# Where a skipped branch's DMAs are issued, and when three bonus terms are: an RWKV and Sinkhorn-MoE kernel on one Trainium2 core

## The chip, the cores and the metric

The kernel runs on one core of one Trainium2 chip. The metric is the device time of one execution in microseconds (us), lower being better; several executions are timed and their median is compared. One further execution is recorded by the hardware profiler. The engines are TensorE (PE, matmuls; its weight loads are PEld), VectorE (DVE), ScalarE (ACT), GpSimd (POOL) and SyncE (SP, which here only issues DMAs). Each engine works through its own instructions in order and waits on semaphores that the others, or landing DMAs, count up.

## The reference

The first half is an RWKV-like recurrence over 768 steps for 4 batches, 8 heads and a head size of 48; the second half a mixture of 8 experts whose gate is normalized by eight Sinkhorn rounds.

```python
def _attn_ref(r, k, v, w, u):
    state = zeros((B, H, D, D))
    for t in range(S):
        cur = einsum('bhd,bhe->bhde', u[None] * kt, vt)
        y[:, :, t] = einsum('bhd,bhde->bhe', rt, state + cur)
        state = w[None, :, :, None] * state + einsum('bhd,bhe->bhde', kt, vt)

def _moe_ref(x, w_gate, w1, w2):          # x: 3072 x 384
    P = exp(x @ w_gate - max)
    for _ in range(8):
        P /= P.sum(1, keepdims=True) + 1e-09
        P /= P.sum(0, keepdims=True) + 1e-09
        P *= N / E
    for e in range(E):
        out += P[:, e:e + 1] * (maximum(x @ w1[e], 0.0) @ w2[e])
```

The decay w is drawn between 0.85 and 0.95.

## The kernel before

**The tiles.** The 3072 tokens are 24 tiles of 128, six to a batch. In the recurrence a tile is one chunk: within it the recurrence becomes a masked matrix product with powers of w, and a state S (48 x 48 per head) is carried from chunk to chunk. For tile tt the code issues these steps, always in the order in which they stand in the text, since every engine is wrapped so that its instructions keep program order:

- `prep` (line 522): POOL scales r to `rp`, DVE scales k to `kp`.
- `bonus_dot` (528): POOL multiplies r by k and by u into `rk`.
- `stage_b` (547): PE transposes rp and kp (`prT`, `pkT`), ACT copies them to `rT` and `kT`.
- `stage_c` (558): PE makes the scores `pA`, DVE copies them under the mask into `at` (COPY_PREDICATED); then PE makes the chunk's state part `pu`, DVE adds it into S, and POOL multiplies S by the chunk's decay `wbd` (two instructions; not in a batch's first chunk).
- `bonus` (537): DVE reduces rk to `dg`, POOL multiplies v by it (into the same buffer, still named rk) and adds `xadd(tt)`, a part of `hbx` that holds zeros unless the branch below has filled it.
- `stage_d` (602): PE makes the output `py`, DVE adds the bonus to give x, takes its largest value and a power-of-two scale.
- `emit` (775): ACT and DVE split x into two fp16 halves (`xsc`), and SP issues a DMA transpose into `hbx`, from where the expert matmuls (`pht`) read it.

**The weights.** `load_part` and `load_w1` issue loads on SP's queue; w1 of the first expert comes in three pieces of 512 KB. DVE takes each piece's largest value (`wm`); a scale follows over PE (`pmax_w`), and ACT and DVE split the weights into two fp16 parts (`ws`). These pieces of work are put in between by `steps(n)`. `spin(n)` issues n filler matmuls on zeros (`pz`).

**The branch.** The closed form is used for channels whose w lies between 0.7 and 1.1. Others are counted in `flag`, and `with tc.If(bad > 0)` (line 487) runs `scan_channels` (443), a loop over all 768 steps that fills `xadd`. With the inputs of this case no channel is outside and the body is never run. Still its DMAs are part of the program: one of w, seven in the loop, and 24 that read `xadd` back, all on SP's queue. Every engine passes the branch on its own: it loads the flag (line 486) and compares (487). For instructions that come later, the body counts as a writer of `xadd`.

**The order at the head.** Lines 791 to 858 issue tiles 0 to 3 by hand, with weight steps and the first expert matmuls in between; from line 860 on a loop goes over the other tiles. In lines 816 to 849 each of the tiles 1 to 3 is issued as `state_of`, `stage_c`, `bonus`; in the loop `bonus` stands ahead of `stage_c`. The expert stages (14 half experts, from line 1294 on) follow.

Of the kernel before, what the change touches and what calls it, by code (L numbers as in the profile page):

```python
# [32 lines left out]
def rwkv_sinkhorn_moe(  # L33
# [13 lines left out]
    V, S_, G, T, Q = (  # L47
        InOrder(tc, e) for e in (nc.vector, nc.scalar, nc.gpsimd, nc.tensor, nc.sync)
    )

    B, H, S, D = r.shape
# [34 lines left out]
    def part(home, dtype, at, shape):  # L86

        n = 1
        for s_ in shape:
            n *= s_  # L90
        x_ = home if home.dtype == dtype else home.bitcast(dtype)
        x_ = x_[:, at : at + n]
        if len(shape) == 1:
            return x_
        names = "abcd"[: len(shape)]
        return x_.rearrange(
            f"p ({' '.join(names)}) -> p {' '.join(names)}", **{c_: s_ for c_, s_ in zip(names[1:], shape[1:])}
        )
# [14 lines left out]
    def xadd(t):  # L113
        return part(hbx, F32, t * DM, (DM,))
# [163 lines left out]
    def whole(gen):  # L278
        leave()
        for _ in gen:  # L280
            pass
# [23 lines left out]
    def spin(n):  # L305
        pz = ps2.tile([P, TB], F32, tag="po", name="pz")
        for _ in range(n):
            T.matmul(pz, zeros[:, :P], zeros, start=True, stop=True)
# [4 lines left out]
    def load_part(tt, nm, src):  # L313
        b, c = divmod(tt, NCHB)
        if tt == 3 and nm != "v":
            t_ = part(hb3, F32, HB + "rk".index(nm) * H * D, (H, D))
        else:
            t_ = ld.tile([P, H, D], F32, tag=nm + "n", name=f"{nm}n_{tt}", bufs=5 if nm == "v" else 3)
        Q.dma_start(t_, src[b, :, c * C : (c + 1) * C, :].rearrange("h t d -> t h d"))
        loads.setdefault(tt, {})[nm] = t_  # L320
# [9 lines left out]
    def load_w1(c):  # L330
        Q.dma_start(raws[0][:, c], w1[0, c * P : (c + 1) * P, :])

    for tt in range(2):
        load_part(tt, "r", r)
        load_part(tt, "k", k)
    load_w1(0)
    load_w1(1)
    load_part(0, "v", v)
    Q.dma_start(
        ub.rearrange("p h d -> p (h d)"),  # L340
        u.rearrange("(o h) d -> o (h d)", o=1).broadcast_to([P, H * D]),
    )
    load_w1(2)
    load_part(1, "v", v)
    load_part(2, "r", r)
# [97 lines left out]
    def scan_channels(scratch):  # L443

        BH = B * H
        yd = scratch.tile([B, S, DM], F32, name="yd")
        rows = [part(hbx, F32, i * BH * D, (BH, D))[:D] for i in range(4)]
        kb, rb, stt, kv = rows
        wn, wbad, wz = (part(hbx, F32, 4 * BH * D + i * H * D, (H * D,))[:D] for i in range(3))
        vt, yv = (part(hbx, F32, 5 * BH * D + i * BH, (BH,))[:D] for i in range(2))  # L450
        Q.dma_start(wn, w.rearrange("(o h) d -> o (h d)", o=1).broadcast_to([D, H * D]))
        V.tensor_scalar(wbad, wn, W_MAX, W_MIN, op0=ALU.min, op1=ALU.max)
        V.tensor_tensor(wbad, wn, wbad, op=ALU.not_equal)
        V.memset(wz, 0.0)
        V.copy_predicated(wz, wbad.bitcast(I32), wn)
        V.memset(stt, 0.0)

        def of_b(x_):
            return x_.rearrange("p (b h) d -> p b (h d)", b=B)

        def for_b(x_):
            return x_.unsqueeze(1).broadcast_to([D, B, H * D])

        with tc.For_i(0, S, 1) as t:
            for dst, src in ((kb, k), (rb, r)):
                Q.dma_start(
                    dst,
                    src.rearrange("b h s d -> s (b h) d")[bass.ds(t, 1)].broadcast_to([D, BH, D]),
                )
            Q.dma_start(vt, v.rearrange("b h s d -> s d (b h)")[bass.ds(t, 1)].rearrange("o d a -> (o d) a"))  # L470
            V.tensor_tensor(rb, rb, stt, op=ALU.mult)
            V.tensor_reduce(yv, rb, axis=AX.X, op=ALU.add)
            for b in range(B):
                Q.dma_start(
                    yd[b].rearrange("s (h d) -> s d h", d=D)[bass.ds(t, 1)].rearrange("o d h -> (o d) h"),
                    yv[:, b * H : (b + 1) * H],
                )
            V.tensor_tensor(of_b(kb), of_b(kb), for_b(wbad), op=ALU.mult)
            V.tensor_tensor(kv, kb, vt.unsqueeze(2).broadcast_to([D, BH, D]), op=ALU.mult)
            V.tensor_tensor(of_b(stt), of_b(stt), for_b(wz), op=ALU.mult)  # L480
            V.tensor_tensor(stt, stt, kv, op=ALU.add)
        yt = yd.rearrange("b s d -> (b s) d").rearrange("(t p) d -> p t d", p=P)
        for t in range(NTT):
            Q.dma_start(xadd(t), yt[:, t, :])

    bad = nc.values_load(flag.bitcast(I32), min_val=0, max_val=0x44000000)
    with tc.If(bad > 0):
        with tc.tile_pool(name="scratch", bufs=1, space=bass.MemoryType.DRAM) as scratch:
            scan_channels(scratch)
# [17 lines left out]
    def gate_across():  # L507
        res = over_partitions(wgm, 1, ps1, "ph", "wg")
        next(res)
        return res  # L510
# [26 lines left out]
    def bonus(tt):  # L537
        vn = loads[tt]["v"]
        dg = at2.tile([P, H], F32, tag="dg", name=f"dg_{tt}")
        V.tensor_reduce(dg, st[tt]["rk"], axis=AX.X, op=ALU.add)  # L540
        av = st[tt].pop("rk")
        G.tensor_tensor(av, vn, dg.unsqueeze(2).broadcast_to([P, H, D]), op=ALU.mult)
        aq = av.rearrange("p h d -> p (h d)")
        G.tensor_tensor(aq, aq, xadd(tt), op=ALU.add)
        st[tt]["av"] = av

    def stage_b(tt):
        d = st[tt]
        for nm, src in (("rT", rp_[tt % 2]), ("kT", kp_[tt % 3])):
            pt = ps3.tile([P, NPAIR, P], F32, tag="pa", name=f"p{nm}_{tt}")  # L550
            sv = src.rearrange("p (a j) d -> p a (j d)", j=2)
            for p_ in range(NPAIR):
                T.transpose(pt[:, p_, :], sv[:, p_, :], ident)
            dst = at2.tile([P, NPAIR, P], F32, tag=nm, name=f"{nm}_{tt}", bufs=3 if nm == "rT" else 2)
            S_.copy(dst, pt)
            d[nm] = dst
# [197 lines left out]
    def work(n, ready=True):  # L754
        if not ready:
            spin(3)
            return
        for _ in range(n):
            if units:
                whole(units.pop(0))  # L760
# [19 lines left out]
    def steps(n):  # L780
        for _ in range(n):
            prepare()
# [4 lines left out]
    def state_of(tt):  # L787
        if ("S", tt) in st:
            st[tt]["S"] = st.pop(("S", tt))
# [23 lines left out]
    gate_max()  # L813
    steps(2)
    spin(3)
    state_of(1)
    stage_c(1)
    bonus(1)
    gate_res = gate_across()
    emit(0)  # L820
    steps(2)
# [7 lines left out]
    gate_split(gate_res)  # L829
    stage_b(3)  # L830
    work(1)
    state_of(2)
    stage_c(2)
    bonus(2)
    work(1)
    emit(1)
    steps(3)
# [6 lines left out]
    stage_d(2)  # L844
    stage_b(4)
    work(1)
    state_of(3)
    stage_c(3)
    bonus(3)
    work(1)  # L850
    steps(1)
    emit(2)
# [489 lines left out]
```

## Time and profile before

| what | value |
|---|---|
| time, median of 3 executions | 1570.2 us (1569.58 to 1573.74) |
| time of the profiled execution | 1572.32 us |
| its span | 1570.6 us, 26412 instructions |
| busy: PE, DVE, ACT, POOL | 97%, 66%, 42%, 38% |
| mean granted clock of PE | 0.985 |
| DMA | 143.14 MB, mean 91 GB/s |

Busy shares are those of the span. In a timeline row stand start, duration, engine, line, operation, output and inputs by the program's names, shape, count, and in brackets the idle time of the engine before it and who ended that. Since the helper class records every instruction, nearly all have the line L29 and are told apart by their names. SPq, POOLq and so on are an engine's sequencer, which issues DMAs and handles branches and semaphores. In a row of waits stand the total, the number and the longest. "Landing" is the time from a DMA's issue to its end.

### The profile page before, as it was taken

Reading aid. Unit: us, or ns where it says so; the run is one execution under the profiler, and the core shown is the slowest. Engines: PE = TensorE matmul, PEld = TensorE weight load, DVE = VectorE, ACT = ScalarE, POOL = GpSimd, SP = SyncE. Lnnn points to the kernel's source line nnn. Section 1 sums busy time; section 2 is a strip of 40 time slices with the busy share of each in tenths; the row PEclk is TensorE's granted clock in tenths of the full one; section 3 lists DMA queues with packets and bytes.
Section 4 is the critical chain, followed back from the end, with each engine's and each line's share of the span. In section 5 each row is a group of like instructions: output and inputs, shape, how many; then the busy total and the mean of one; then the engine's idle time right before and its main releaser. Section 6 shows DMA issues by size and latency. Waiting matters only on the chain.

```text
span 1570.6 us, 26412 instructions
## 1 busy us (share of the span) xinstructions
PE 1526.4 (97%) x10435; PEld 869.3 (55%) x10435; DVE 1029.6 (66%) x1715; ACT 663.6 (42%) x1164; POOL 596.9 (38%) x712
## 2 busy tenths in 40 slices
PE   6689999999999999999999999999999999999999
PEld 3666676555555555555555555555555555555555
DVE  6568877867656666666666666766666666656554
ACT  3133342444535454444445454545444444535320
POOL 5557997601022424334242425242333424242200
PEclk8799999999999999999999999999999999999999
DMA  7244551321135566666666666564545554555434
GB/s 182 52 93 103 109 118 49 107 81 39 56 100 106 60 89 123 89 126 90 118 86 122 89 119 96 79 109 60 96 58 98 59 96 60 96 60 96 56 91 131
DMA packets 186846, 143.14 MB, mean 91 GB/s; under 512 B 109536, under 2 KB 180960, under 8 KB 186720
## 3 DMA queue, kind: packets, MB, share of 16 engines
q0 software_dynamic: 44928, 61.36, 31.8%
q1 hardware_dynamic: 141584, 80.07, 18.6%
q8 instruction: 82, 1.34, 0.4%
q14 instruction: 44, 0.36, 0.1%
q10 hardware_dynamic: 208, 0.00, 0.0%
HBM read 55.39 MB, written 80.23 MB: 86 GB/s over the span
## 4 chain that ended last, share of the span: by engine, by line
PE 89%; DVE 4%; POOL 4%; issue 1%; ACT 0%; DMA 0%; POOLq 0%; DVEq 0%
PE po L29 46%; PE bZ L29 11%; PE bY L29 11%; PE bA L29 5%; PE bB L29 5%; PE ph L29 4%; PE bC L29 2%; POOL rk L29 2%; PE py L29 1%; PE pA L29 1%; PE pht L29 1%; POOL ws L29 1%; POOL rp L29 1%; DVE ws L29 1%; DVE hb L29 0%
## 5 line engine op out<-in xcount | busy, mean ns | idle before, releaser
L29 PE MATMUL po<-ws,hbx 128*128 128x384 f16 x3360 | 736.8, 326 | 0.0
L29 POOL DMA_DIRECT2D accd<-stg x288 | 250.4, 870 | 694.9 <-ACT stg L29 676.5
L29 PEld LDWEIGHTS <-hbx 128*128 128x128 f16 x3504 | 334.1, 98 | 292.5
L29 PEld LDWEIGHTS <-ws 128*128 128x128 f16 x3240 | 312.4, 100 | 243.9 <-issue 5.4
L29 PE MATMUL po<-ws,hb 128*128 128x384 f16 x1248 | 327.0, 330 | 5.4 <-ACT ws L29 2.5
L29 ACT ACTIVATE hbx<-tb 128x512 f16<-128x512 f32 x224 | 141.1, 630 | 449.6 <-DVE tb L29 449.6
L29 DVE TENSOR_TENSOR tb<-bY,tb 128x512 f32<-128x512 f32 x168 | 116.2, 692 | 195.7 <-PE bY L29 195.5
L29 ACT ACTIVATE stg<-po,pe 128x384 f32<-128x384 f32 x312 | 179.4, 575 | 121.9 <-PE po L29 95.1
L29 PE MATMUL bZ<-xv,ws 128*128 128x512 f16 x840 | 227.0, 379 | 0.4 <-DVE tb L29 0.4
L29 PE MATMUL bY<-xv,ws 128*128 128x512 f16 x840 | 227.0, 379 | 0.0
L29 DVE TENSOR_TENSOR tb<-bZ,tb 128x512 f32<-128x512 f32 x168 | 115.6, 688 | 135.6 <-PE bZ L29 135.6
L29 PEld LDWEIGHTS <-hb 128*128 128x128 f16 x1248 | 122.2, 99 | 101.5 <-issue 7.9
L29 POOL TENSOR_TENSOR ucb<-rawb 128x256 f32<-128x256 f32 x84 | 75.4, 948 | 117.1 <-DMA rawb<-in_moe_w_dram 117.1
L29 DVE TENSOR_TENSOR tb<-bB,tb 128x512 f32<-128x512 f32 x112 | 77.5, 692 | 49.1 <-PE bB L29 47.2
L29 PE MATMUL ph<-hbx,ws 128*128 128x384 f16 x504 | 93.1, 330 | 3.1 <-DMA hbx<-xsc 2.5
L29 DVE SCALAR_TENSOR_TENSOR hb<-tb,hbx 128x512 f16<-128x512 f32 x112 | 77.2, 690 | 24.6 <-ACT hbx L29 19.5
L29 PE MATMUL bA<-xv,ws 128*128 128x512 f16 x336 | 90.8, 379 | 0.0
L29 PE MATMUL bB<-xv,ws 128*128 128x512 f16 x336 | 90.8, 379 | 0.0
L29 DVE SCALAR_TENSOR_TENSOR hbx<-tb,hbx 128x512 f16<-128x512 f32 x112 | 77.9, 696 | 14.7 <-ACT hbx L29 10.4
L29 ACT COPY tb<-bZ 128x512 f32<-128x512 f32 x56 | 32.8, 586 | 65.4 <-PE bZ L29 65.4
L29 ACT COPY stg<-po 128x384 f32<-128x384 f32 x48 | 22.9, 477 | 72.0 <-PE po L29 62.9
L29 DVE TENSOR_REDUCE wms<-rawb 128x1 f32<-128x768 f32 x56 | 51.8, 944 | 0.0
(171 smaller groups left out, 1538.0 us busy)
## 6 DMA issues: line engine op xcount, KB each, us to landing
accd<-stg POOLq DMA_DIRECT2D x288, 192.0 KB, 3.7
rawb<-in_moe_w_dram SPq DMA_DIRECT2D x28, 768.0 KB, 7.2
e0d<-stg SPq DMA_DIRECT2D x48, 192.0 KB, 2.1
hb<-e0d SPq DMA_DIRECT2D x48, 192.0 KB, 3.9
vn<-in_v_dram SPq DMA_DIRECT2D x24, 192.0 KB, 3.3
accd<-stg SPq DMA_DIRECT2D x24, 192.0 KB, 1.8
accd<-hb POOLq DMA_DIRECT2D x24, 192.0 KB, 4.8
rawb<-accd SPq DMA_DIRECT2D x24, 192.0 KB, 2.5
```

The lines of the kernel that those rows point to most:

```text
L29: return lambda *a, **k: self.tc.keep_in_program_order(f(*a, **k))
```

## The change

Three things are changed. All DMAs of the branch body go by GpSimd's queue (`G`) in place of SP's (`Q`). In the loads ahead of the branch, u (`ub`) and v of tile 0 are issued before the second piece of w1. And for tiles 1 to 3 `bonus` is issued before `state_of` and `stage_c`.

```diff
     load_w1(0)
-    load_w1(1)
-    load_part(0, "v", v)
     Q.dma_start(
         ub.rearrange("p h d -> p (h d)"),
         u.rearrange("(o h) d -> o (h d)", o=1).broadcast_to([P, H * D]),
     )
+    load_part(0, "v", v)
+    load_w1(1)
     load_w1(2)
...
-        Q.dma_start(wn, w.rearrange("(o h) d -> o (h d)", o=1).broadcast_to([D, H * D]))
+        G.dma_start(wn, w.rearrange("(o h) d -> o (h d)", o=1).broadcast_to([D, H * D]))
...
             for dst, src in ((kb, k), (rb, r)):
-                Q.dma_start(
+                G.dma_start(
...
-            Q.dma_start(vt, v.rearrange("b h s d -> s d (b h)")[bass.ds(t, 1)].rearrange("o d a -> (o d) a"))
+            G.dma_start(vt, v.rearrange("b h s d -> s d (b h)")[bass.ds(t, 1)].rearrange("o d a -> (o d) a"))
...
             for b in range(B):
-                Q.dma_start(
+                G.dma_start(
                     yd[b].rearrange("s (h d) -> s d h", d=D)[bass.ds(t, 1)].rearrange("o d h -> (o d) h"),
...
         for t in range(NTT):
-            Q.dma_start(xadd(t), yt[:, t, :])
+            G.dma_start(xadd(t), yt[:, t, :])
...
     spin(3)
+    bonus(1)
     state_of(1)
     stage_c(1)
-    bonus(1)
     gate_res = gate_across()
```

Tiles 2 and 3 are changed as tile 1 is, with `bonus` now behind `work(1)` and ahead of `state_of`.

SP's instructions around the branch, of before (-) and after (+), its start; the semaphores in brackets are what an instruction waits for, DMAHW0 to 7 being those of the DMAs that SP and ACT issue:

```order
 L486 TENSOR_LOAD flag [waits DVE_49]
 L487 COMPARE_AND_BRANCH
-L29 DMA hbx<-in_w_dram 48x384 [waits DMAHW4_49,Activation_49]
 L464 COMPARE_AND_BRANCH
-L464 UNCONDITIONAL_BRANCH [waits DMAHW0_49,DMAHW1_49,DMAHW2_49,DMAHW3_49,DMAHW5_49,DMAHW6_49,DMAHW7_49]
```

The body's DMA of w, and with it the waits on the other seven semaphores, leave SP's program; the body's 31 others go in the same way.

POOL's instructions from the bonus of tile 0 to the state of tile 1, with their waits (rk_233 is the buffer of tile 0, rk_348 of tile 1, rk_431 of tile 2; DMASW0 to 7 are the semaphores of the DMAs that POOL issues):

```order
 L29 TENSOR_TENSOR rk_233<-vn_121,dg_387 128x384 [waits DMAHW0_49,DVE_49]
-L29 TENSOR_TENSOR rk_233<-rk_233,hbx 128x384 [waits DMAHW5_49,DMAHW4_49,Pool_49]
-L29 TENSOR_TENSOR rp_197<-rn_127,rtab 128x8x48 [waits PE_49]
-L29 TENSOR_TENSOR rk_431<-rn_127,kn_129 128x384
+L29 TENSOR_TENSOR rk_233<-rk_233,hbx 128x384 [waits DMASW1_49,DMASW0_49,Pool_49]
+L29 TENSOR_TENSOR rp_197<-rn_127,rtab 128x8x48 [waits DMAHW4_49,PE_49]
+L29 TENSOR_TENSOR rk_431<-rn_127,kn_129 128x384 [waits DMAHW5_49]
 L29 TENSOR_TENSOR rk_431<-rk_431,ub 128x384 [waits Pool_49]
+L29 TENSOR_TENSOR rk_348<-vn_125,dg_483 128x384 [waits DMAHW3_49,DVE_49]
+L29 TENSOR_TENSOR rk_348<-rk_348,hbx 128x384 [waits DMASW1_49,Pool_49]
 L29 TENSOR_TENSOR S_205<-S_205,wbd 64x4x48 [waits DVE_49]
 L29 TENSOR_TENSOR S_205<-S_205,wbd 64x4x48 [waits DVE_49,Pool_49]
```

The add of `xadd(0)` (a part of hbx) waits on two of POOL's own DMA semaphores in place of two of SP's, and the two bonus instructions of tile 1 now stand ahead of the state's.

DVE's instructions of tile 1 (at_203 holds its masked scores, S_205 its state; mt_wg and md_wg belong to the gate's scale):

```order
 L29 RECIPROCAL sw_323<-isw_322 128x1
-L29 COPY_PREDICATED at_203<-mask,pA_0_483 128x4x128
-L29 COPY_PREDICATED at_203<-mask,pA_1_484 128x4x128
-L29 TENSOR_TENSOR S_205<-pu_503,S_204 64x4x48 x2
-L29 TENSOR_REDUCE dg_516<-rk_348 128x8
+L29 TENSOR_REDUCE dg_483<-rk_348 128x8
+L29 COPY_PREDICATED at_203<-mask,pA_0_487 128x4x128
+L29 COPY_PREDICATED at_203<-mask,pA_1_488 128x4x128
+L29 TENSOR_TENSOR S_205<-pu_507,S_204 64x4x48 x2
 L29 TENSOR_REDUCE mt_wg<-pmax_wg 1x1
```

The reduce to dg moves from behind the mask copies and the state to ahead of them; in tiles 2 and 3 the same happens.

More of the change, by code (lines that the diff above doesn't have):

```diff
@@ L831, in rwkv_sinkhorn_moe @@
     work(1)
+    bonus(2)
     state_of(2)
     stage_c(2)
-    bonus(2)
     work(1)
@@ L846, in rwkv_sinkhorn_moe @@
     work(1)
+    bonus(3)
     state_of(3)
     stage_c(3)
-    bonus(3)
     work(1)
```

## The prediction

> **What bounds the kernel now.** I read the page first, for where TensorE (PE) is not busy; then the waits of PE by stretches of time; then the timeline of the first 75 us. All times are us from the start of the span.
>
> ```profile
> PE   6689999999999999999999999999999999999999
> ...
> PE prT L29 <- POOL rp L29: 20.2, 4, 8.2
> PE pkT L29 <- DVE kp L29: 2.1, 1, 2.1
> ...
> PE prT L29 <- POOL rp L29: 3.9, 3, 2.0
> ...
> 200.00:300.00 100.00, 99.91 (x1197) 67.67 (x1195) 77.02 (x152) 38.19 (x71) 77.94 (x89) 1.00 0.39 97
> ```
>
> One digit is 39 us. PE is the bound from the third digit on, and in the window of 200 to 300 us it is busy 99.91 of 100. So only time that PE loses at the head can be won. The first two wait rows are for 20 to 75 us: PE waits 20.2 us in four pieces for POOL's `rp` (the scaled r of the next tile, transposed by `prT`). The third row is for 75 to 200 us and is small: 3.9.
>
> The largest piece is 8.2. The timeline shows what POOL did before it:
>
> ```profile
> 16.35 0.83 POOL L29 TENSOR_TENSOR rk<-vn,dg 128x384 f32<-128x384 f32 x1 [0.51 <-DVE dg L29]
> 17.99 1.05 SPq L29 DMA_DIRECT2D vn<-in_v_dram  x1
> 18.49 1.90 PE L29 MATMUL py<-vn,at 128*64 128x48 f32 x32
> 26.58 0.99 POOL L29 TENSOR_TENSOR rk<-rk,hbx 128x384 f32<-128x384 f32 x1 [9.40 <-SPq L487]
> 27.53 1.00 POOL L29 TENSOR_TENSOR rp<-rn,rtab 128x384 f32<-128x384 f32 x1
> 28.58 1.11 PE L29 MATMUL prT<-ident,rp 128*128 128x128 f32 x4 [8.19 <-POOL rp L29]
> ...
> L487 SPq EVENT_SEMAPHORE  x8: 17/17/17, 20.2 to 26.5; - x8
> ...
> vn<-in_v_dram SPq DMA_DIRECT2D x1, 192.0 KB, 8.3
> ```
>
> The If is not taken, yet POOL sits 9.40 us in front of its add of `xadd(0)` until SyncE (SP) is done at line 487. There SP runs eight semaphore events, spread over 20.2 to 26.5. I read them as SP making up the counts that the skipped body would have added to its eight DMA semaphores, each behind the transfer already in flight on that semaphore: the last load before the If (v of tile 3, issued at 17.99, landing 8.3 later) lands at 26.3, and the last event is at 26.5. POOL's add waits on those counts, since the body would have written `xadd`. Behind it in POOL's order stands rp of tile 2, and behind that PE.
>
> **The change part by part.**
>
> *The branch body on GpSimd's queue.* The counts to be made up are now those of POOL's own DMA semaphores, which no instruction before the If uses, so there is nothing in flight to wait for, and POOL comes to them early: I take nothing for them. SP no longer waits at line 487. What is late next for PE is `py` of tile 0, which ends at 18.49 + 1.90 = 20.39. POOL's add would run at about 17.2, rp of tile 2 a us later (both inputs landed), so neither holds PE.
>
> *The order of the loads.* It has a price on VectorE (DVE):
>
> ```profile
> 12.24 1.21 DVE L29 TENSOR_REDUCE wm<-ws 128x1 f32<-128x1024 f32 x1
> 12.78 1.02 POOL L29 TENSOR_TENSOR rk<-rk,ub 128x384 f32<-128x384 f32 x1 [1.19 <-DMA ub<-in_u_dram]
> ```
>
> The reduce at 12.24 reads w1's second piece. The three transfers are swapped within the same bytes, so that piece now lands about where u did, shortly before 12.78. DVE starts that reduce 0.4 us later, and the mask copies, dg of tile 0 and py behind it too: +0.4. POOL's 1.19 for u goes, but its next step waited 0.51 for DVE's dg anyway (row at 16.35), so nothing is won by it. Bounds: 0 to +1.2, one such reduce.
>
> So PE goes on at 20.8 in place of 28.58: 7.8 us won (bounds 7.0 to 8.2). It also goes on warm:
>
> ```profile
> 13.82 0.66 PE L29 MATMUL prT<-ident,rp 128*128 128x128 f32 x4
> 17.75 0.81 PE L29 MATMUL pz<-zeros 128*128 128x512 f16 x3
> 32.34 1.10 PE L29 MATMUL pA<-rT,kT 64*64 64x128 f32 x32
> 28.60:32.40 3.80, 3.80 (x17) 2.38 (x18) 1.17 (x8) 1.90 (x3) 1.88 (x2) 0.52 1.13 220
> ```
>
> After 8.2 idle us the granted clock was 0.52 for 28.6 to 32.4, and from prT to pA took 32.34 - 28.58 = 3.76. Warm, the four steps between are prT 0.66, pkT about 0.6, a small matmul with its issue 0.4, and the filler pz 0.81: 2.5. That wins 1.25 more, and pA of tile 1 starts at 23.3 (bounds 0.6, if the clock falls in between, to 1.3).
>
> *The bonus of tile 1 ahead of its mask.*
>
> ```profile
> 33.55 1.36 DVE L29 COPY_PREDICATED at<-mask,pA 128x512 f32<-128x512 int32 x2 [1.91 <-PE pA L29]
> 35.56 0.55 DVE L29 TENSOR_REDUCE dg<-rk 128x8 f32<-128x384 f32 x1
> 36.54 5.26 POOL L29 TENSOR_TENSOR rk<-vn,dg 128x384 f32<-128x384 f32 x1
> 36.59 0.60 DVE L29 SCALAR_TENSOR_TENSOR xsc<-x,xs,xsc 128x384 f16<-128x384 f32 x1
> 37.11 3.53 DVE L29 SCALAR_TENSOR_TENSOR ws<-ws,sw,ws 128x1536 f16<-128x1536 f32 x2
> 40.57 0.54 DVE L29 TENSOR_TENSOR kp<-hb,ktab 128x384 f32<-128x384 f32 x1
> 42.91 0.56 DVE L29 TENSOR_TENSOR x<-py,rk 128x384 f32<-128x384 f32 x1 [1.80 <-POOL rk L29]
> 43.88 1.11 PE L29 MATMUL prT<-ident,rp 128*128 128x128 f32 x4 [6.79 <-POOL rp L29]
> 45.85 3.72 PE pht L29 x36
> ```
>
> POOL's product, 0.83 us in the row at 16.35, took 5.26 here: it stands still while DVE runs two-input instructions without a break from 36.59 to 41.11. After the change dg runs in the 1.91 us in which DVE waits for pA, and POOL does product and add long before. The mask copies shift with pA to 24.5, and DVE's run ends 41.11 - 33.55 = 7.56 less the 0.58 from dg to the next instruction, that is at 31.5 with kp and at 32.05 with x, whose input is now ready. But rp of tile 3 is now the POOL instruction that meets that run (it comes up at about 27.4). I let it stand still to the end of x and take 1.0: PE's prT at 33.1 in place of 43.88, 10.8 ahead. This part wins 10.8 - 9.05 = 1.75 (bounds 1.0, if POOL recovers 0.7 late, as it did here at 41.80 after 41.11, and 3.4, in the first rival).
>
> [...]
>
> The matmuls pht at 45.85 also need the DMA transpose of tile 0, which now queues behind the six loads of tiles 4 and 5 that SP issues from about 20.7. Those moved at 220 GB/s (window row above): 6 x 196,608 bytes take 5.4 us from 26.3 on, to 31.7.
>
> ```profile
> hbx<-xsc SPq DMA_TRANSPOSE x1, 2.6
> ```
>
> With 2.6 for the transpose itself it lands by 34.3, before PE gets to pht at 33.1 + 1.97 = 35.0. So it is hidden, by 0.7.
>
> *The bonuses of tiles 2 and 3.*
>
> ```profile
> 55.68 0.99 POOL L29 TENSOR_TENSOR rp<-rn,rtab 128x384 f32<-128x384 f32 x1
> 58.76 0.54 DVE L29 TENSOR_TENSOR kp<-kn,ktab 128x384 f32<-128x384 f32 x1
> 59.45 1.01 PE L29 MATMUL pkT<-ident,kp 128*128 128x128 f32 x4 [2.07 <-DVE kp L29]
> 69.82 2.58 POOL L29 TENSOR_TENSOR rp<-rn,rtab 128x384 f32<-128x384 f32 x2
> 71.18 1.12 PE L29 MATMUL prT<-ident,rp 128*128 128x128 f32 x4 [3.57 <-POOL rp L29]
> 73.15 3.72 PE pht L29 x36
> ```
>
> In tile 2, rp at 55.68 moves up by two POOL steps, but pkT then still waits for kp, the end of DVE's unbroken row, which loses only dg (0.58) and perhaps some port waiting: 0.8 (0.5 to 1.0). In tile 3, rp starts after POOL's state product, at about 67.7 in place of 69.82, and kp moves up by dg and more: prT and pkT could come 2.4 earlier. The transpose of tile 2 then comes last, about 2.0 earlier than pht at 73.15: I take 2.2 (1.5 to 2.5).
>
> *Sum:* 7.8 + 1.25 + 1.75 + 0.8 + 2.2 = 13.8. Behind tile 3 I see nothing that gives it back: the waits up to 200 us are for POOL, DVE and transposes that all start from earlier work of the same chain, and the loads have long landed. The profiled execution took 1572.32 (span 1570.6), so it would take 1558.5. The median of the three runs is 1570.2, and I forecast against that: 1570.2 - 13.8 = 1556.4.
>
> **The rivals.**
>
> 1. *More is won* (25%). [...]
>
> ```profile
> 55.10:56.70 1.60, 0.00 (x0) 0.00 (x0) 1.60 (x2) 0.00 (x0) 1.60 (x3) 1.00 0.41 96
> 67.60:71.20 3.60, 0.03 (x2) 0.03 (x1) 3.60 (x7) 0.51 (x1) 3.44 (x5) 0.80 0.24 55
> ```
>
> A gap of 1.60 left the clock at 1.00, one of 3.60 brought it to 0.80 and the following pht to 3.72. (Busy times of PE, PEld, DVE, ACT and POOL, then the granted clock.) If the second gap shrinks to about 1.5, pht runs at about twice the pace and some 1.5 more is won. Time 1554.7 by the first way (10%), 1554.9 by the second (15%), 1553.2 by both.
>
> 2. *The transpose of tile 0 is late* (13%): SP's issue of the loads stalls, or the loads go slower with v of tile 3 and w2 in flight. If it lands at 37 in place of 34.3, PE loses 2.0: 1558.4; at 39, 1560.4. For it: it is hidden by only 0.7.
>
> 3. *The wait stays* (6%): POOL's add is still held by the loads. Then only 1.75 + 0.8 + 2.2 = 4.75 are won: 1565.4.
>
> 4. *Slower* (2%): POOL itself is held at line 487 as SP was. It passes there before its first rp at 9.29, on which everything hangs. Held to SP's 26.5 it would shift the head by 17.2, PE's prT of tile 2 to some 37.6, 9.0 later than now, and PE, idle that long, would run its next steps at the low clock as it does at 28.58, 1.25 more; less 4.75 that is 5.5 lost: 1575.7. It decides from a hold to about 21 on. Against it: no transfer before the If counts on POOL's semaphores.
>
> The other 4% are for what I don't see.
>
> **How the numbers follow.** My sum has 50%: 1556.4. The terms' low bounds together (7.0, 0.6, 1.0, 0.5, 1.5) make 10.6, 1559.6; the first rival in full 1553.2; with the second rival and the three runs' spread of 4 us the range is 1551.5 to 1562. A measurement of this kernel tells about 0.3% (4.7 us) from no change. Faster by more than that are the sum, rivals 1 and 2 and half of 3 and of the rest: 0.93; same 0.05; slower 0.02.
>
> **What would show it.** POOL's add of `xadd(0)` at 17 to 18 without a wait; no spread of events on SP at line 487; prT of tile 2 at about 20.8; pA of tile 1 at 23.3; prT of tile 3 at about 33 and pht at 35, with POOL's rp, not rk, the long instruction beside DVE's run. I am wrong if prT of tile 2 comes later than 22, if pht of tile 0 waits for the DMA, or if PE's idle time grows by several us behind 75 us.

## The result, and the profile after

| | before | after |
|---|---|---|
| time, median of 5 executions | 1570.88 us (1569.58 to 1573.77) | 1559.05 us (1556.46 to 1562.16) |
| ratio after / before, 95% interval | | 0.992 (0.9899 to 0.9942) |
| profiled execution, its span | 1572.32 us, 1570.6 us | 1559.05 us, 1557.5 us |
| mean granted clock of PE in it | 0.985 | 0.990 |

The change makes the kernel 0.8% faster: 11.8 us by the medians, 13.3 by the profiled executions. The forecast was 13.8 and 1556.4 us, with a range of 1551.5 to 1562.0.

The views of the profile after follow in the order of those before: the page's slices, the waits of PE (20 to 75 us first, then one row of 75 to 200 us), line 487, the timeline.

```profile
PE   6799999999999999999999999999999999999999
```

```profile
PE pkT L29 <- DVE kp L29: 7.7, 2, 4.8
...
PE prT L29 <- POOL rp L29: 2.3, 2, 1.4
PE pht L29 <- DMA hbx<-xsc: 0.5, 1, 0.5
...
PE prT L29 <- POOL rp L29: 3.9, 3, 2.0
```

PE's 20.2 us of waiting for `rp` at the head have become 2.3. In their place `kp` (DVE's scaled k) is waited for 7.7 us in two pieces, where it was 2.1 in one. Behind 75 us the row of 3.9 is as it was. Of the other waits in 20 to 75 us only one is long, 2.4 us of `po` for ACT's `ws`, and it stood behind 75 us before (2.5). So nothing was given back.

The instructions of line 487, with duration and first and last start:

```profile
L487 POOLq EVENT_SEMAPHORE  x4: 17/43/43, 7.5 to 7.7; - x4
...
L487 POOLq INC_SWDGE_SEM  x1: 177/177/177, 7.8 to 7.8; - x1
...
L487 SPq COMPARE_BRANCH  x1: 45/45/45, 20.3 to 20.3; - x1
```

SP's eight events over 20.2 to 26.5 are gone, and SP passes the If in one comparison. POOL has five short instructions of its own at that line, all before 8 us; I read them as its own counts being made up. The timeline of tile 0 and the start of tile 1:

```profile
17.54 0.83 POOL L29 TENSOR_TENSOR rk<-vn,dg 128x384 f32<-128x384 f32 x1 [2.06 <-DVE dg L29]
18.45 0.99 POOL L29 TENSOR_TENSOR rk<-rk,hbx 128x384 f32<-128x384 f32 x1
...
19.68 1.95 PE L29 MATMUL py<-vn,at 128*64 128x48 f32 x32
...
21.56 1.12 PE L29 MATMUL prT<-ident,rp 128*128 128x128 f32 x4
...
24.35 1.10 PE L29 MATMUL pA<-rT,kT 64*64 64x128 f32 x32
```

The add of `xadd(0)` at 18.45 follows the product without the wait of 9.40, PE goes from py straight to prT of tile 2, and pA of tile 1 starts at 24.35 in place of 32.34.

Four starts on PE cut the head into the terms of the forecast's sum. They are read from each kernel's timeline, in us:

| kernel | pA of tile 1 | pht of tile 0 | pht of tile 1 | pht of tile 2 |
|---|---|---|---|---|
| before | 32.34 | 45.64 | 60.25 | 72.94 |
| after | 24.35 | 36.14 | 49.63 | 60.36 |
| won on the way, after | 7.99 | 1.51 | 1.12 | 1.96 |
| forecast of it | 9.05 | 1.75 | 0.8 | 2.2 |
| only the branch | 22.87 | 36.17 | 50.02 | 63.80 |
| only the bonuses | 32.70 | 44.74 | 57.59 | 68.15 |
| only the loads | 32.86 | 47.03 | 60.67 | 74.38 |
| all but the loads | 23.45 | 35.24 | 48.86 | 59.61 |

The terms add up to 12.58 us at pht of tile 2; the spans differ by 13.1. So the time was won where it was forecast, and three of four terms lie within 0.35 us. Each row is one execution, though: in the bonus-only kernel the last three steps are 1.26, 1.76 and 2.13, so a single step is good to some 0.6 us. The last four rows are experiments, told next.

### The profile page after: what moved, and what is told of

The parts are those of the page before. It is cut to its first block, busy times and chain, and to the rows that moved or that the text cites. A ratio compares the mean times of both kernels' runs of the same rounds, so it can differ in the third digit from the quotient of the medians.

```text
span 1557.5 us, 26474 instructions
## 1 busy us (share of the span) xinstructions
PE 1524.6 (98%) x10435; PEld 867.5 (56%) x10435; DVE 1031.3 (66%) x1715; ACT 662.8 (43%) x1164; POOL 596.2 (38%) x712
## 3 DMA queue, kind: packets, MB, share of 16 engines
q8 instruction: 82, 1.34, 0.4%
## 4 chain that ended last, share of the span: by engine, by line
PE 90%; DVE 5%; POOL 3%; issue 1%; DMA 0%; ACT 0%; SPq 0%; POOLq 0%; DVEq 0%
PE po L29 47%; PE bZ L29 12%; PE bY L29 12%; PE bA L29 5%; PE bB L29 5%; PE ph L29 4%; PE bC L29 2%; PE py L29 2%; POOL rk L29 1%; PE pA L29 1%; PE pht L29 1%; DVE ws L29 1%; POOL ws L29 1%; DVE hb L29 0%; DVE at L29 0%
```

## The experiments

**Theory and rivals.** The theory: two parts each win by themselves, the branch through SP's wait at line 487, the bonuses through a meeting of DVE's and POOL's instructions, and the load order wins nothing. (A meeting is what the rows show: two-input instructions of DVE and POOL overlap in time, and one or both take longer. In before, POOL's product takes 5.26 us beside DVE's run from 36.59 on, and 0.83 at 16.35.) The rivals: the wait isn't that of transfers in flight; the bonuses win nothing once the wait is gone; what holds POOL at 36.54 is the operand that it repeats over each head, not the moment.

**One part of the change at a time** (all against the kernel before; 1572.13 us in these runs).

Only the branch's DMAs go by GpSimd's queue; loads and bonuses are as before.

```diff
-            Q.dma_start(xadd(t), yt[:, t, :])
+            G.dma_start(xadd(t), yt[:, t, :])
```

> Only the branch body's DMAs go by GpSimd's queue; loads and bonus terms stand as before. My theory: the removed wait at the branch is the large part. POOL's add of xadd(0) comes at 17 to 18 without a wait, PE's prT of tile 2 at 20.4 to 20.9 and pA of tile 1 about 9 us ahead of 32.34, while POOL's product of tile 1 still stands still for 4 us or more beside DVE's run: 1570.9 - 9 = 1562. Rival: the parts cover each other, and without the early bonus the same POOL stall gives part of the 9 back: 1566 or more.

Measured: 1561.11 us (1557.02 to 1562.46), ratio 0.9926 (0.9911 to 0.9941); applied to 1572.13, the ratio makes 11.6 us. The timeline of this kernel at tile 1:

```profile
27.08 5.25 POOL L29 TENSOR_TENSOR rk<-vn,dg 128x384 f32<-128x384 f32 x1
27.11 0.60 DVE L29 SCALAR_TENSOR_TENSOR xsc<-x,xs,xsc 128x384 f16<-128x384 f32 x1
27.64 3.53 DVE L29 SCALAR_TENSOR_TENSOR ws<-ws,sw,ws 128x1536 f16<-128x1536 f32 x2
...
34.41 1.12 PE L29 MATMUL prT<-ident,rp 128*128 128x128 f32 x4 [6.79 <-POOL rp L29]
```

The wait at the branch is gone: pA of tile 1 comes 9.47 us earlier. (Two things work against each other in that number: POOL's first rp starts at 10.53 here and at 9.29 in before, and py and prT run in 1.14 and 0.66 us where the whole change has 1.95 and 1.12.) The meeting of the two engines is untouched, with POOL's product standing still for 5.25 us and PE waiting the same 6.79 as before. At pht of tile 2 the kernel is 9.14 ahead, which is the theory's 9; the ratio's 2.5 more come later, and are taken up with the last of these four.

Only the bonuses of tiles 1 to 3 ahead of state and mask.

```diff
-    state_of(1)
-    stage_c(1)
     bonus(1)
+    state_of(1)
+    stage_c(1)
```

> Only the bonus terms of tiles 1 to 3 are issued ahead of their masks; the branch body and the loads stand as before. My theory: POOL still waits 9 us at the branch, prT of tile 2 stays at 28.6, and 1.75 + 0.8 + 2.2 = 4.75 are won behind it: 1566. Rival: the wait at the branch leaves POOL so late that the early bonus of tile 1 finds no gap (POOL is busy with rk of tile 2 until 30.6), and only tiles 2 and 3 give something: 1568.

Measured: 1566.53 us (1563.68 to 1569.8), ratio 0.9964 (0.9949 to 0.9979), by the ratio 5.7 us. Its timeline:

```profile
28.90 1.11 PE L29 MATMUL prT<-ident,rp 128*128 128x128 f32 x4 [8.51 <-POOL rp L29]
...
43.85 1.09 PE L29 MATMUL pkT<-ident,kp 128*128 128x128 f32 x4 [4.80 <-DVE kp L29]
```

The wait at the branch is there in full (8.51), and 4.79 us are won behind it, against 4.75 in the forecast's sum. So the bonuses win by themselves. The second row shows that the 4.80 us of waiting for kp come with them.

Only the order of the loads.

```diff
-    load_w1(1)
-    load_part(0, "v", v)
     Q.dma_start(ub...)
+    load_part(0, "v", v)
+    load_w1(1)
```

> Only the order of the loads is changed (u and v of tile 0 ahead of w1's second piece). My theory: nothing on the path while the wait at the branch stands; DVE's second reduce starts 0.4 to 1.2 later, dg of tile 0 too, and the 9 us wait behind it takes that up: 1570.9, no change. Rival: the swap itself wins by starting POOL's product with u 1 us earlier: 1570; or it delays py of tile 0 past the wait: no, that needs 6 us.

Measured: 1572.87 us (1569.2 to 1575.13), ratio 1.0002 (0.9991 to 1.0013): no change. In its one trace pht of tile 2 is 1.44 later than in before all the same; 0.9 of that is pA of tile 1, which ran in 1.99 us where before has 1.10.

The branch and the bonuses, with the loads in the old order.

```diff
-    load_part(0, "v", v)
     load_w1(1)
+    load_part(0, "v", v)
+    Q.dma_start(ub...)
```

> Branch body on GpSimd's queue and the bonus terms early, but the loads in the old order. My theory: the load order costs what the profile after shows, py of tile 0 1.0 us later at the same start; without it pA of tile 1 comes 0.5 to 1.2 us earlier and the time is that of the changed kernel less about 1: 1558. Rival: the load order wins 0.5 to 1, since POOL has u and v earlier: 1560.

Measured: 1558.48 us (1558.25 to 1560.43), ratio 0.9914 (0.99 to 0.9928), by the ratio 13.5 us. That is not told apart from the whole change (0.992). By the table it reaches pht of tile 2 0.75 us sooner than the whole change.

By the ratios the parts don't add up: 11.6 + 5.7 = 17.3 against 13.5. In the head they do: 9.14 + 4.79 = 13.93 against 72.94 - 59.61 = 13.33. What is over lies behind the head, and the granted clock shows a part of it. The timeline of before, of the whole change and of the branch alone at the same nine matmuls, and the window around them in the last two (length, PE's busy time and count, granted clock, DMA share, GB/s):

```profile
117.83 3.04 PE L29 MATMUL ph<-hbx,ws 128*128 128x384 f16 x9 [2.46 <-DMA hbx<-xsc]
```

```profile
105.23 3.06 PE L29 MATMUL ph<-hbx,ws 128*128 128x384 f16 x9 [2.56 <-DMA hbx<-xsc]
...
105.00:115.00 10.00, 9.77 (x133) 0.83 0.33 72
```

```profile
107.04 1.64 PE L29 MATMUL ph<-hbx,ws 128*128 128x384 f16 x9 [2.40 <-DMA hbx<-xsc]
...
105.00:115.00 10.00, 7.96 (x131) 1.00 0.52 120
```

After nearly the same wait the clock fell in two of these executions and not in the third, for 1.4 us. Once more, between 155 and 175 us, the first two show a window of 0.83 and the third none. From pht of tile 2 to the span's end before takes 1497.7, the whole change 1497.1, the branch alone 1493.9. Of the 3.8 us by which the branch alone is shorter there, two windows at 0.83 make 2 x 0.17 x 10 = 3.4. So it has them from its clock rather than from the edit, as far as these single profiles show; that its other executions did the same is not shown. In all 13 profiles the stretch from pht of tile 2 to the end takes 1492.6 to 1497.8.

**What the wait at the branch waits for.** The body stays on SP's queue, as before, but w2 and v of tile 3, the last two loads before the If, are issued behind it.

```diff
-    Q.dma_start(raws[1], w2[0].rearrange("(c p) d -> p c d", p=P))
-    load_part(3, "v", v)
...
             scan_channels(scratch)
 
+    Q.dma_start(raws[1], w2[0].rearrange("(c p) d -> p c d", p=P))
+    load_part(3, "v", v)
     spin(4)
```

> The kernel before, with the loads of w2 and of v of tile 3 issued behind the If in place of ahead of it; the branch body stays on SP's queue. My theory: SP's eight events at the branch each wait for the transfer in flight on their semaphore, so the last one now follows the landing of k of tile 3 (about 21), POOL's add of xadd(0) comes at 21 to 21.5 in place of 26.6, and PE's prT of tile 2 at about 23.2 in place of 28.6. Rival: the events cost SP some 6 us by themselves, or wait for something else than the loads: then the last event still stands 6 to 7 us behind SP's compare, and the add at 24 or later.

Measured in one execution: 1563.64 us beside 1572.59 (median) for before. The landing of the load that is now the last before the If (k of tile 3), and the timeline:

```profile
hb<-in_k_dram SPq DMA_DIRECT2D x1, 192.0 KB, 3.6
```

```profile
17.52 0.79 SPq L29 DMA_DIRECT2D hb<-in_k_dram  x1
...
21.46 0.99 POOL L29 TENSOR_TENSOR rk<-rk,hbx 128x384 f32<-128x384 f32 x1 [3.74 <-SPq L485]
...
23.46 1.12 PE L29 MATMUL prT<-ident,rp 128*128 128x128 f32 x4 [3.06 <-POOL rp L29]
```

That load is issued at 17.52 and lands 3.6 later, at 21.1, and POOL is released at 21.46. Without any change to the branch, its wait ends 5.1 us sooner than in before, where it ended with v of tile 3. This settles it: the skipped body makes its queue wait for what is in flight there.

**What holds PE at pkT in the changed kernel.** Three kernels change the order around the meetings of DVE and POOL. First, kp of tile 3 and of tile 4 are made ahead of the weights' splits (`steps`) in place of behind them; `prep` then leaves them out.

```diff
     emit(0)
+    prep_k(3)
     steps(2)
...
     emit(1)
+    prep_k(4)
     steps(3)
```

> The changed kernel, with DVE's scaling of k (kp) of tiles 3 and 4 issued right after the x split of tiles 0 and 1, ahead of the weight splits and maxima that it waits behind in the profile after (PE's pkT waits 4.8 and 2.9 for it). My theory: kp is now what bounds these two tiles, and moving it wins up to 1.9 in tile 3 (then the transpose of tile 0, landing at 34.1, comes last) and up to 2.4 in tile 4: 4 less than the changed kernel, ratio to the kernel before about 0.9895. Rival: pkT's wait is only the first of several that end together (weight split, transpose, POOL), and no more than 1 is won: ratio 0.992.

Measured: 1554.62 us (1553.47 to 1555.89), ratio 0.9888 (0.9871 to 0.9906). The timeline:

```profile
30.54 0.63 PE L29 MATMUL pkT<-ident,kp 128*128 128x128 f32 x4
...
34.76 4.00 PE L29 MATMUL pht<-hbx,ws 128*128 128x128 f16 x36 [3.60 <-DMA hbx<-xsc]
```

pkT runs 4.7 us sooner, but pht of tile 0 only 1.4 sooner: it now waits 3.60 for the transpose. This is the wait that the forecast's second rival is about, and it stood right behind kp.

Next, the same with the three loads of tile 5 moved behind the transpose of tile 0.

```diff
-    load_chunk(5)
     bonus_dot(2)
...
+    load_chunk(5)
     load_chunk(6)
     bonus_dot(3)
```

> As the run before it in this list, and the loads of tile 5 are issued behind the transpose of tile 0. My theory: with kp out of the way the transpose's place in the queue counts: it lands at about 32 in place of 34.1, pht of tile 0 follows the weight split at 32.2, and 1 to 2 more are won: ratio 0.9885. Rival: the transpose takes its 3.8 wherever it stands, or the split is later than that: no difference to the run before.

Measured: 1553.15 us (1552.96 to 1553.26), ratio 0.9881 (0.9865 to 0.9898). Its timeline:

```profile
32.16 0.27 PE L29 MATMUL pht<-hbx,ws 128*128 128x128 f16 x2 [0.78 <-DMA hbx<-xsc]
33.15 2.07 PE L29 MATMUL pht<-hbx,ws 128*128 128x128 f16 x34 [0.73 <-DVE ws L29]
```

The wait of 3.60 falls to 0.78, and the next one, 0.73, is for the split weights themselves. The time goes the way of the expectation, but by the ratios the step from the kernel before it (1.5 us) lies inside the intervals, though all four executions are below that kernel's four. Pht of tile 0 starts at 32.16, 2.6 earlier.

Then, by itself on the changed kernel: POOL's two products of r, k and u of tile 3 (`bonus_dot`) are moved off DVE's splits. If it is they that make DVE late, the splits should take 3.5 to 4.5 in place of 5.03 and kp 0.54 in place of 1.34, with pkT at 33.0 to 34, pht at about 34.2 and a ratio of 0.9905.

```diff
-    bonus_dot(3)
...
     bonus(2)
+    bonus_dot(3)
     state_of(2)
```

> The changed kernel, with POOL's two products of r, k and u of tile 3 issued behind the bonus of tile 2, so that POOL has only rp of tile 3 to do while DVE splits the weights. [...]

Measured: 1554.37 us (1553.7 to 1555.11), ratio 0.9891 (0.9874 to 0.9908). The timeline:

```profile
30.16 4.27 DVE L29 SCALAR_TENSOR_TENSOR ws<-ws,sw,ws 128x1536 f16<-128x1536 f32 x2
34.35 0.55 DVE L29 TENSOR_TENSOR kp<-hb,ktab 128x384 f32<-128x384 f32 x1
...
35.05 1.09 PE L29 MATMUL pkT<-ident,kp 128*128 128x128 f32 x4 [3.25 <-DVE kp L29]
```

Without the two products the splits take 4.27 in place of 5.03 and kp 0.55 in place of 1.34, and PE waits 3.25 in place of 4.80. It is POOL that makes DVE late here. The time doesn't price the edit: by the ratios it is 4.5 us below the changed kernel, but pht of tile 2 starts only 0.81 earlier (59.55). The rest lies behind it and stays open; the mean granted clock is 0.993 in this execution and 0.990 in the changed kernel's.

**All together.** The three edits in one kernel, with the new and with the old order of the loads.

```diff
     emit(0)
+    prep_k(3)
     steps(2)
+    load_chunk(5)
     load_chunk(6)
-    bonus_dot(3)
...
     bonus(2)
+    bonus_dot(3)
```

> The changed kernel with all three further edits: kp of tiles 3 and 4 early, the loads of tile 5 behind the transpose of tile 0, POOL's products of tile 3 behind the bonus of tile 2. My theory: each takes away a wait that stood last in turn, so that they add up in part: pht of tile 0 starts when the transpose lands (32.2) and doesn't wait for the weight split (0.73) or x (0.5): 1 to 2 less than with the first two alone, ratio 0.987. Rival: PE's next waits (rp of tile 5, the w2 split) take it up: ratio 0.988 or more.

> As the run before it in this list, with the loads in the old order (w1's second piece ahead of u and v of tile 0). My theory: the new order costs 0.4 to 0.8 on DVE's second reduce, so this one is 0.4 to 0.8 faster: ratio 0.9866. Rival: the order makes no difference that shows: the same ratio; or it wins: 0.9875.

Measured: 1552.78 us (1550.0 to 1556.04), ratio 0.9883 (0.9864 to 0.9903), and with the old loads 1551.89 us (1551.31 to 1554.5), ratio 0.9879 (0.9859 to 0.99). Neither is told apart from the kernel with early kp and early transpose (0.9881), so the further gains that were expected (0.987 and 0.9866) are not shown. By the start of pht of tile 2 the five kernels stand at 57.54 (early kp), 54.98 (transpose), 59.55 (products), 55.77 (all) and 54.54 (all, old loads), against 60.36 for the changed one. The timeline of the first of the two shows a new wait:

```profile
45.73 0.66 PE L29 MATMUL prT<-ident,rp 128*128 128x128 f32 x4 [2.59 <-POOL rp L29]
```

The moved products now stand ahead of rp of the next tile on POOL, and PE waits 2.59 for that, where the kernel with early kp and early transpose has 0.62. That is a part of why the edits don't add up. Another is the head of this one execution: pht of tile 0 starts at 33.79 in place of 32.16, since pA of tile 1 came 0.76 later and took 1.99 in place of 1.10. The version with the old loads has the lowest median. It beats the kernel before by 1.2% (1.0 to 1.4%) and, by the two ratios, the changed kernel by some 0.4%, with intervals that just touch.

**Operand or moment.** The branch-only kernel, where POOL's product of tile 1 reads the plain tile `ub` in place of dg repeated over each head. This kernel leaves out the true bonus term of tile 1, so only its timeline is of use. If the moment decides and not the operand, the product should still take about 5.

```diff
-        G.tensor_tensor(av, vn, dg.unsqueeze(2).broadcast_to([P, H, D]), op=ALU.mult)
+        G.tensor_tensor(av, vn, ub, op=ALU.mult)
```

> The kernel with the branch body on GpSimd's queue alone (bonus terms late, old loads), in which POOL's product of v and dg of tile 1 reads u, a plain tile, in place of dg, a broadcast operand; tile 1's bonus term is thus another one. It asks why that product stood still for 5.25 while rp and the products of tile 3 took turns with DVE's instructions. Theory of the operand: with a plain tile it takes turns too, lasts 2.6 or less, and the splits are stretched from 3.53 to over 4. [...]

Measured in one execution: 1565.92 us. The timeline:

```profile
30.88 5.43 POOL L29 TENSOR_TENSOR rk<-vn,ub 128x384 f32<-128x384 f32 x1
30.93 0.60 DVE L29 SCALAR_TENSOR_TENSOR xsc<-x,xs,xsc 128x384 f16<-128x384 f32 x1
31.45 3.53 DVE L29 SCALAR_TENSOR_TENSOR ws<-ws,sw,ws 128x1536 f16<-128x1536 f32 x2
```

With a plain operand the product stands still as long (5.43), and the rival of the operand falls. Tile 2 speaks for the moment at which the product comes up: there the same product meets the same split of x. In the branch-only kernel:

```profile
43.30 0.83 POOL L29 TENSOR_TENSOR rk<-vn,dg 128x384 f32<-128x384 f32 x1
43.52 1.03 DVE L29 SCALAR_TENSOR_TENSOR xsc<-x,xs,xsc 128x384 f16<-128x384 f32 x1
```

Here POOL is 0.22 ahead, not 0.03. It runs in 0.83, and it is DVE that takes longer, 1.03 in place of 0.60. Four traces with the late bonuses (before, the branch alone, two loads late, the plain operand) have both meetings: a lead of 0.03 to 0.05 in tile 1 with 5.25 to 5.43 on POOL, and one of 0.21 or 0.22 in tile 2 with 0.83.

## Why the prediction was right, and where a step was not

**The wait at the branch, 7.8 us: right, and 7.02 as measured.** PE's prT of tile 2 came at 21.56 in place of 28.58, at the low end of the bounds. The add ran without a wait, behind a dg that came later than forecast, SP's events are gone, and the experiment with two loads behind the If shows their cause. Rivals 3 (the wait stays) and 4 (POOL itself is held) fell: POOL passes line 487 by 8 us.

**The term of tile 0 as a whole, 9.05: too large by 1.06.** Mis-sized were "+0.4" for the later load, with which 0.78 of the 1.06 went, and 2.5 for the steps from prT to pA, with the other 0.28. py ended at 21.63, 1.24 later than before and not 0.4. The forecast let DVE wait for w1's second piece. That landed about where the forecast had it, at 12.6 (issued at 6.21, and 6.4 to landing), but DVE was busy until 13.46; the price came by another way, since with u early POOL's product with u runs beside DVE's kp:

```profile
12.12 0.99 POOL L29 TENSOR_TENSOR rk<-rk,ub 128x384 f32<-128x384 f32 x1
12.35 1.19 DVE L29 TENSOR_TENSOR kp<-kn,ktab 128x384 f32<-128x384 f32 x1
13.46 1.21 DVE L29 TENSOR_REDUCE wm<-ws 128x1 f32<-128x1024 f32 x1
```

The reduce of that piece follows kp at once; kp itself takes 1.19. With the old loads, and the rest changed, the same row reads 0.55:

```profile
12.05 0.55 DVE L29 TENSOR_TENSOR kp<-kn,ktab 128x384 f32<-128x384 f32 x1
```

That is 0.64 of the 1.24, and it is the load order's: kp of tile 1 takes 1.19 in five kernels with the new order (the whole change, kp early, transpose first, late products, all together) and 0.54 or 0.55 in six with the old (before, the branch alone, the bonuses alone, all but the loads, two loads late, the plain operand). Another 0.57 was there before kp began (12.35 against 11.78). It comes from the start of the chain: POOL's first rp runs at 9.88 in place of 9.29, behind 14 filler matmuls of PE that took 3.58 us in place of 3.19. Those fillers start at 5.17 in three traces with the branch on GpSimd's queue (the whole change, the branch alone, all but the loads) and at 4.96 in before; the rest goes with the single execution, for that rp starts anywhere from 9.29 (before) to 10.53 (the branch alone) and 10.58 (all together), with no order by the other edits. The kernel with the old loads has pA of tile 1 0.90 earlier (23.45), of which 0.29 is such a start (9.59). From prT to pA took 24.35 - 21.56 = 2.79, with prT at 1.12 where the forecast had a warm 0.66: PE came from py without a gap, but the granted clock was 0.51 over 19.6 to 21.6 and 0.73 over 21.56 to 24.35.

**The bonus of tile 1, 1.75: right in size, wrong in its step.** The step that failed is "I let it stand still to the end of x", of rp of tile 3. The timeline:

```profile
24.16 0.53 DVE L29 TENSOR_REDUCE dg<-rk 128x8 f32<-128x384 f32 x1
...
24.77 0.83 POOL L29 TENSOR_TENSOR rk<-vn,dg 128x384 f32<-128x384 f32 x1 [2.02 <-DVE dg L29]
...
27.23 1.25 POOL L29 TENSOR_TENSOR S<-S,wbd 64x192 f32<-64x192 f32 x2 [0.54 <-DVE S L29]
...
28.02 0.88 DVE L29 SCALAR_TENSOR_TENSOR xsc<-x,xs,xsc 128x384 f16<-128x384 f32 x1
28.56 1.19 POOL L29 TENSOR_TENSOR rp<-hb,rtab 128x384 f32<-128x384 f32 x1
28.82 5.03 DVE L29 SCALAR_TENSOR_TENSOR ws<-ws,sw,ws 128x1536 f16<-128x1536 f32 x2
29.71 2.52 POOL L29 TENSOR_TENSOR rk<-hb 128x384 f32<-128x384 f32 x1
29.80 0.66 PE L29 MATMUL prT<-ident,rp 128*128 128x128 f32 x4 [0.87 <-POOL rp L29]
...
32.31 2.39 POOL L29 TENSOR_TENSOR rk<-rk,ub 128x384 f32<-128x384 f32 x1
33.78 1.34 DVE L29 TENSOR_TENSOR kp<-hb,ktab 128x384 f32<-128x384 f32 x1
...
35.27 1.08 PE L29 MATMUL pkT<-ident,kp 128*128 128x128 f32 x4 [4.80 <-DVE kp L29]
36.14 4.05 PE L29 MATMUL pht<-hbx,ws 128*128 128x128 f16 x36
```

dg, product and add run early, as forecast. That rp stands still so long was the author's estimate from the one row of 5.26; here it takes 1.19, not five, and prT comes at 29.80. The first way of rival 1 was such an rp: run at 27.4, ahead of DVE's run, with pht at 33.3 and 1.7 us more won. That gain didn't come with it. POOL's next two products overlap DVE's splits, and both sides take longer: 2.52 and 2.39 on POOL in place of 1.01 and 1.00 in before, 5.03 for the splits in place of 3.53 and 1.34 for kp in place of 0.54 on DVE. So kp is late instead of rp, and pht starts at 36.14 where the forecast, which counted from 1.06 earlier, had 35.0. The kernels with early kp and with late products each move this wait, which shows that kp is the cause. That the forecast's mechanism, a late rp, and the real one, a late kp, come to nearly one number (1.75 and 1.51) was luck.

**The transpose of tile 0: hidden, as forecast.** It landed at 34.1 (issued at 30.33, and 3.8 by the row below) against "by 34.3".

```profile
hbx<-xsc SPq DMA_TRANSPOSE x1, 3.8
```

The sum holds by two errors that cancel: the forecast had 31.7 and 2.6. And half of rival 2 did happen, since SP's issue of the loads stalled: two of the six took 4.35 and 2.13 us to issue, where in before none of these six took over 1.07, and the transpose was issued 1.4 after `xsc` was ready (28.90). The late kp hid that. Where kp comes early it shows: 3.60 us of waiting.

**Tiles 2 and 3, 0.8 and 2.2: right.** They won 1.12 (its bound was 1.0) and 1.96. No run shows the "port waiting" that the forecast put into the 0.8; in its place they show the split of x of that tile at 1.03 in before, beside POOL's product, and at 0.71 in after. In tile 2 kp remains the last, and in tile 3 the transpose comes last by 0.54, both as forecast:

```profile
49.17 0.63 PE L29 MATMUL pkT<-ident,kp 128*128 128x128 f32 x4 [2.91 <-DVE kp L29]
...
60.36 3.81 PE L29 MATMUL pht<-hbx,ws 128*128 128x128 f16 x36 [0.54 <-DMA hbx<-xsc]
```

The second way of rival 1, a pht at about twice the pace in tile 3, did not happen here (3.81); in the bonus-only kernel it did (2.17).

**The median, 2.65 us above the forecast.** 0.7 of it is the median before, which was 1570.2 in the first three executions and 1570.88 in all five. Another 1.2 is what the head came short (12.58 in place of 13.8). The five executions of after, from 1556.46 to 1562.16, go with their mean granted clock (0.992 in the two fastest, 0.989 in the two slowest), so the median alone doesn't test a term of 1 us; the starts in the timeline do.

## What to carry to other kernels

A branch that is never taken can still cost, here 9.40 us of POOL's waiting: look in the trace at the line of the If for semaphore events spread over time, and put the body's DMAs on a queue that has nothing in flight there (PE's prT came at 21.56 in place of 28.58). When instructions of two engines hold each other up, as POOL's product at 5.26 in place of 0.83 us did here, moving one out of the meeting can move the next one into it (2.52 and 2.39 in place of 1.01 and 1.00), so read which instruction comes up then, on both engines, and price the delay on both sides. Judge edits of about a microsecond by the starts of landmarks in the trace, since whole executions differ by more (the five of after by 5.7 us, with mean granted clocks from 0.989 to 0.992). The clock and the start of the chain move landmarks too (the 36 matmuls of one pht took 2.17 to 4.05 us here, in after 2.18 at a granted clock of 1.00 and 4.05 at 0.51), so compare the steps between them, and in more than one kernel.

## What the runs showed of the hardware that had not been expected

**A lead of 0.05 us that didn't help POOL, and one of 0.2 that did.** In four traces (before, the branch alone, two loads late, the plain operand) a product on POOL came up 0.03 to 0.05 us ahead of DVE's run of four two-input instructions. It then took 5.25 to 5.43 us and ended 0.7 to 0.9 us behind the end of DVE's run, whose splits took 0.60 and 3.53 in all four (the whole change has 0.88 and 5.03). With a lead of 0.21 or 0.22 in tile 2 of the same traces the product took its 0.83, and DVE's split of x 1.03 in place of 0.60. The plain operand's 5.43 shows nothing won by another operand. That the lead decides is a reading of these two groups of values; no run has this product at a lead between 0.05 and 0.21. In after, POOL's S was already under way (27.23 to 28.48) when DVE's run began at 28.02, and then instructions of both engines took longer (on POOL 1.19, 2.52 and 2.39 where before has 1.00, 1.01 and 1.00; on DVE 0.88, 5.03 and 1.34 where it has 0.60, 3.53 and 0.54). Why POOL's product doesn't end between the four DVE instructions in tile 1 of the four traces stays open; it wasn't tried with DVE's run delayed.

**A clock that drops behind a wait of about 2.5 us in some executions.** Nine matmuls took 3.04 us in before and 3.06 in after behind waits of 2.46 and 2.56, and 1.64 in the branch-only kernel behind one of 2.40. The window of 10 us around them showed a granted clock of 0.83 in before and after and 1.00 in the branch-only kernel. An estimate from these windows is 0.17 x 10 = 1.7 us lost at the clock, beside 1.4 by which the nine matmuls differ. The length of the wait alone doesn't decide: the same nine took 3.06 behind 2.39 in the kernel with early kp and 1.64 behind 2.40 in the one with late products. What does is not shown.

**A load order that costs through a meeting.** Two transfers issued earlier did not make DVE wait for another; they let POOL's product with u (12.12 to 13.11) and DVE's kp (from 12.35 on) meet, and kp took 1.19 us in place of 0.55. No difference in the kernel's time was shown for it.
